# Replacing the scheduler's order by one written by hand in the first fifth of a fused attention and mixture-of-experts kernel

## The chip, the cores and the metric

The kernel runs on one NeuronCore of a Trainium2 chip. The metric is the device time of one execution in microseconds (us). PE is the matrix engine, DVE the vector engine, ACT the scalar engine, POOL the GpSimd engine, and SP the engine that only issues transfers. Each engine executes its own queue in order, and waits on semaphores for the others.

## The reference

Eight batches (B) of 512 tokens (S) and a state of 32 rows (Ns), with 8 heads (H) of 64 columns (D). The tokens read the state, the state reads the tokens, and the 8 x 544 rows go through 8 experts (E) with 1024 hidden columns (F), all experts for all rows, weighted by a matrix P that eight Sinkhorn rounds normalise:

```python
a = softmax(scale * x @ state.T)        # per batch and head: (512, 32)
xread = a @ state
a2 = softmax(scale * state @ x.T)       # (32, 512)
sread = a2 @ x
X = concatenate([xread, sread], axis=2) # as (4352, 512) rows
P = exp(X @ w_gate - max)
for _ in range(8):
    P /= P.sum(1, keepdims=True) + 1e-09
    P /= P.sum(0, keepdims=True) + 1e-09
    P *= N / E
out = sum over e of P[:, e:e+1] * (maximum(X @ w1[e], 0) @ w2[e])
```

## The kernel before

**Attention, in halves.** A batch's eight heads are done as two groups of four (`q` = 0, 1; in the code NQ = 2). The 16 groups are called heads below. For one head, PE transposes x (8 matmuls of 128 columns into `xT_ps`), DVE copies them out (`xT`), PE makes the scores (2 of 512 columns, `sc_ps`), ACT takes the exponential (`E2`, with its row sums), PE sums over state rows (`den_ps`), ACT makes the reciprocal with Ln and Exp (`rcp`), DVE divides the rows (`rrec`, `En`), PE transposes `En` (`ET_ps`), DVE copies that (`ET`) and multiplies `AT`, the weights with which tokens read the state, and PE reads x with `ET` (`su_ps`), which DVE copies to `xs`. `AT` and `xs` are all that the rest needs: X itself is never formed. `gate` multiplies a batch's `AT` with state x gate weights and ACT takes the exponential into `Pmat`.

**Expert 0.** For a pair of batches, `state_times_w1` forms state x W1 (8 matmuls into `g_ps`, each copied out in two halves to `G`). `layer1(c)` multiplies `G` with `AT` of batch c (8 steps of 2 matmuls into `hps`; ACT writes `hT` with Relu), `layer2(0, c)` multiplies `hT` with W2 (4 tiles of 8 matmuls into `yps`, copied to `acc`). c = 8 stands for the 256 state rows.

**Sinkhorn and experts 1 to 7.** A Sinkhorn round is a chain: four DVE instructions on `Pmat` that end in `cpart`, one small matmul (`csb_ps`), two DVE instructions. It can start only when all batches have been through `gate`. After it, `acc` (34 tiles) is multiplied by column 0 of `Pmat` (line 348), and experts 1 to 7 add to it. Their second layer is a seven-product (Winograd) scheme: `w2_sums` makes four sums of W2 (`wt`), `sums` four sums of `hT` (`sm`), and each product's tile (`ra`, `rb`, `rc`) is added to `acc` by DVE with a factor from `Pmat` (line 364).

**What sets the order.** The program is written phase by phase: all attention, Sinkhorn, expert 0, experts 1 to 7, with `merge` interleaving steps of two layers. The tile framework then schedules: it tracks every dependency, places tiles in pools, and interleaves the phases on each engine by its own priorities. SBUF is shared in time: the second weight buffer `moe_w1` is a pool opened after the attention pools are closed (`actx.close()`, line 255), so the load of expert 1's weights waits for the last head. PSUM has 8 banks: 4 for attention (`psA`) and 4 for the experts (`psM`), later all 8 (`psW`). Transfers of x and state go by SP's queue, transfers of weights by POOL's, which casts to 16 bits on the way; POOL also casts x of batches 1 to 7 (line 96), DVE that of batch 0.

Of the kernel before, what the change touches and what calls it, by code (L numbers as in the profile page):

```python
# [18 lines left out]
def kernel(  # L19
# [32 lines left out]
    mw = [ctx.enter_context(tc.tile_pool(name="moe_w0", bufs=1)), None]  # L52
    mh = ctx.enter_context(tc.tile_pool(name="moe_h", bufs=3))
# [32 lines left out]
    load_state(0)  # L86

    def load_x(b):
        x_nat = axp.tile([128, NKC, NSC, 2, D], FP16, name="x_nat", tag="x_nat")
        xv = x[b].rearrange("h (p s) d -> p h s d", s=NSC)  # L90
        for q in range(NQ):
            x_st = axs.tile([128, 4, NSC, D], FP32, name="x_st", tag="x_st")
            nc.sync.dma_start(out=x_st, in_=xv[:, ds(4 * q, 4)])
            for par in range(2):
                eng = nc.vector if b == 0 else nc.gpsimd
                eng.tensor_copy(out=x_nat[:, 2 * q + par].rearrange("p s i d -> p i s d"),
                                in_=x_st[:, ds(2 * par, 2)])
        return x_nat

    def load_w(e, after=None):  # L100
        w1h = mw[e % 2].tile([128, NKC, F], FP16, name="w1h", tag="w1h")
        w2h = mw[e % 2].tile([128, NFB, Dm], FP16, name="w2h", tag="w2h")
        for g in range(2):
            fs = ds(F // 2 * g, F // 2)
            if after is not None and g == 0:

                nc.gpsimd.tensor_copy(out=w1h[:1, 0, :1], in_=after[:1, 0, 0, 0, :1])
            nc.gpsimd.dma_start(out=w1h[:, :, fs], in_=w1r[e, :, :, fs])
# [18 lines left out]
    identh = consts.tile([128, 128], FP16, name="identh")  # L127
    make_identity(nc, identh)
    headones = consts.tile([128, 128], FP16, name="headones")
    nc.vector.memset(headones, 0.0)  # L130
    for h in range(4):
        nc.vector.memset(headones[ds(32 * h, 32), ds(32 * h, 32)], 1.0)
    nc.gpsimd.memset(stT, 0.0)
    ones128 = consts.tile([128, 128], FP32, name="ones128")
    nc.gpsimd.memset(ones128, 1.0)
    wgh = consts.tile([128, NKC, E], FP16, name="wgh")
    nc.gpsimd.dma_start(out=wgh, in_=moe_w_gate.rearrange("(kc p) e -> p kc e", p=128))

# [15 lines left out]
    x_nats = [load_x(0)]  # L154
    prepare_state(0)
    w_cur = load_w(0, x_nats[0])
    load_state(1)
    x_nats.append(load_x(1))

    def attention(b):  # L160
        xn = x_nats[b]
        odd = b % 2
        for q in range(NQ):
            xT_ps = psA.tile([128, 2, S], FP16, name="xT_ps", tag="a")
            for par in range(2):
                for sc in range(NSC):
                    nc.tensor.transpose(xT_ps[:, par, ds(128 * sc, 128)],
                                        xn[:, 2 * q + par, sc, :, :], identh)
            xT = asb.tile([128, 2, S], FP16, name="xT", tag="xT")
            nc.vector.tensor_copy(out=xT, in_=xT_ps)  # L170
            sc_ps = psA.tile([128, S], FP32, name="sc_ps", tag="a")
            for par in range(2):
                nc.tensor.matmul(sc_ps[ds(64 * (par ^ odd), 64), :],  # L173
                                 stT[:, b // 2, 2 * q + par, par ^ odd, :], xT[:, par, :])
            E2 = asb.tile([128, S], FP16, name="E2", tag="E2")
            rowsum = asb.tile([128, 1], FP32, name="rowsum", tag="rowsum")
            nc.scalar.activation(out=E2, in_=sc_ps, func=AF.Exp, scale=inv_sqrt_d,
                                 accum_out=rowsum)
            den_ps = psA.tile([128, S], FP32, name="den_ps", tag="a")
            nc.tensor.matmul(den_ps, headones, E2)  # L180
            lnd = asb.tile([128, S], FP32, name="lnd", tag="lnd")
            nc.scalar.activation(out=lnd, in_=den_ps, func=AF.Ln)  # L182
            rcp = asb.tile([128, S], FP16, name="rcp", tag="rcp")
            nc.scalar.activation(out=rcp, in_=lnd, func=AF.Exp, scale=-1.0)
            rrec = asb.tile([128, 1], FP32, name="rrec", tag="rrec")
            nc.vector.reciprocal(out=rrec, in_=rowsum)
            En = asb.tile([128, S], FP16, name="En", tag="En")
            nc.vector.tensor_scalar(out=En, in0=E2, scalar1=rrec, scalar2=None, op0=ALU.mult)
            ET_ps = psA.tile([128, NSC, 128], FP16, name="ET_ps", tag="a")
            for sc in range(NSC):  # L190
                nc.tensor.transpose(ET_ps[:, sc, :], En[:, ds(128 * sc, 128)], identh)
            ET = asb.tile([128, NSC, 128], FP16, name="ET", tag="ET")
            nc.vector.tensor_copy(out=ET, in_=ET_ps)
            nc.vector.tensor_mul(AT[:, q, ds(b * S, S)], E2, rcp)
            su_ps = psA.tile([128, 2, 64], FP32, name="su_ps", tag="a")
            for par in range(2):
                for sc in range(NSC):
                    nc.tensor.matmul(su_ps[:, par, :], xn[:, 2 * q + par, sc, :, :],
                                     ET[:, sc, ds(64 * (par ^ odd), 64)],
                                     start=(sc == 0), stop=(sc == NSC - 1))  # L200
            for i in range(2):
                nc.vector.tensor_copy(
                    out=xs[ds(64 * i, 64), ds(2 * q, 2), ds(b * Ns, Ns)],
# [295 lines left out]
```

## Time and profile before

| | |
|---|---|
| runs, median (lowest to highest) | 826.42 us (825.89 to 826.93), n = 4 |
| profiled execution: time, span of the core | 826.72 us, 824.9 us |
| busy in the span: PE, DVE, ACT, POOL | 789.8, 627.1, 614.0, 44.8 us |
| chain that ended last | PE 82%, DVE 9%, ACT 4%, DMA 3% |
| bytes read from and written to HBM | 42.48 MB, 8.91 MB |

Times inside the profile count from the first instruction (0) to the last (824.9); the 1.8 us between that and 826.72 lie around them. "Busy" of PE is the time in which some matmul was under way: matmuls are pipelined, so a PE that is shown busy can still be waiting between two. In groups of instructions a row gives the line, engine, operation, output and inputs, shapes and count, then busy time and mean duration, then the idle time of the engine just before them and what ended it. In a timeline a row gives the start, the length and the engine, and in brackets the idle time before and its releaser.

### The profile page before, as it was taken

Reading aid. Unit: us, or ns where it says so; the run is one execution under the profiler, and the core shown is the slowest. Engines: PE = TensorE matmul, PEld = TensorE weight load, DVE = VectorE, ACT = ScalarE, POOL = GpSimd, SP = SyncE. Lnnn points to the kernel's source line nnn. Section 1 sums busy time; section 2 is a strip of 40 time slices with the busy share of each in tenths; the row PEclk is TensorE's granted clock in tenths of the full one; section 3 lists DMA queues with packets and bytes.
Section 4 is the critical chain, followed back from the end, with each engine's and each line's share of the span. In section 5 each row is a group of like instructions: output and inputs, shape, how many; then the busy total and the mean of one; then the engine's idle time right before and its main releaser. Section 6 shows DMA issues by size and latency. Waiting matters only on the chain.

```text
span 824.9 us, 14279 instructions
## 1 busy us (share of the span) xinstructions
PE 789.8 (96%) x5584; PEld 518.8 (63%) x5584; DVE 627.1 (76%) x1353; ACT 614.0 (74%) x1158; POOL 44.8 (5%) x70
## 2 busy tenths in 40 slices
PE   3999979999999999999999999999999999999997
PEld 1344433456767667776667666776667666776664
DVE  3565768868887888788877888788877988788873
ACT  2687845698886788778886788878886788778861
POOL 3322010100000000000000000000000000000000
PEclk9999999999999999999999999999999999999999
DMA  9730060150003300060003300060003300003223
GB/s 197 212 103 27 1 102 1 22 80 3 1 1 53 52 1 1 1 102 2 2 1 52 52 1 1 2 102 1 1 1 52 52 1 2 1 14 116 102 104 103
DMA packets 33108, 35.53 MB, mean 43 GB/s; under 512 B 4112, under 2 KB 28688, under 8 KB 33040
## 3 DMA queue, kind: packets, MB, share of 16 engines
q0 software_dynamic: 17424, 16.79, 13.3%
q1 hardware_dynamic: 15616, 17.83, 6.6%
q8 instruction: 43, 0.70, 0.4%
q14 instruction: 25, 0.20, 0.1%
HBM read 42.48 MB, written 8.91 MB: 62 GB/s over the span
## 4 chain that ended last, share of the span: by engine, by line
PE 82%; DVE 9%; ACT 4%; DMA 3%; issue 1%; POOL 0%; SPq 0%; POOLq 0%
PE hps L298 24%; PE ra L358 24%; PE rc L358 12%; PE yps L315 6%; PE g_ps L237 6%; PE rb L358 5%; PE hps L303 2%; ACT hT L305 2%; DMA w2h<-in_moe_w_dram 1%; DMA w1h<-in_moe_w_dram 1%; DVE acc L364 1%; DVE sm L342 1%; DVE G L240 1%; PE sc_ps L173 1%; ACT lnd L182 1%
## 5 line engine op out<-in xcount | busy, mean ns | idle before, releaser
L305 ACT ACTIVATE hT<-hps 128x512 f16<-128x512 f32 (+1 forms) x576 | 306.7, 574 | 91.7 <-PE hps L298 62.6
L240 ACT CAST G<-g_ps 64x512 f16<-64x512 f32 x480 | 276.8, 577 | 65.2 <-PE g_ps L237 62.4
L298 PE MATMUL hps<-AT,G 128*128 128x512 f16 x1024 | 281.4, 383 | 2.0 <-ACT G L240 1.0
L364 DVE SCALAR_TENSOR_TENSOR acc<-ra,Pmat,acc 128x256 f32<-128x256 f32 x464 | 217.6, 479 | 46.7 <-PE ra L358 46.2
L358 PEld LDWEIGHTS <-sm 128*128 128x128 f16 x1856 | 178.9, 97 | 76.6 <-issue 14.8
L358 PEld LDWEIGHTS <-hT 128*128 128x128 f16 x1392 | 135.8, 98 | 51.3 <-issue 5.8
L298 PEld LDWEIGHTS <-G 128*128 128x128 f16 x1024 | 100.0, 99 | 72.7 <-issue 6.9
L358 PE MATMUL ra<-wt,sm 128*128 128x256 f16 x928 | 139.2, 272 | 3.2 <-DVE acc L364 2.4
L364 DVE SCALAR_TENSOR_TENSOR acc<-rc,Pmat,acc 128x256 f32<-128x256 f32 x232 | 111.5, 480 | 38.3 <-PE rc L358 38.2
L237 PE MATMUL g_ps<-w1h,stT 128*128 128x512 f16 x256 | 97.7, 388 | 5.0 <-DMA w1h<-in_moe_w_dram 3.9
L315 PE MATMUL yps<-w2h,hT 128*128 128x512 f16 x320 | 79.4, 382 | 0.6 <-ACT hT L305 0.4
L358 PE MATMUL ra<-w2h,hT 128*128 128x256 f16 x464 | 75.2, 273 | 0.0
L358 PE MATMUL rc<-wt,sm 128*128 128x256 f16 x464 | 70.6, 273 | 0.0
L358 PE MATMUL rb<-w2h,hT 128*128 128x256 f16 x464 | 69.7, 273 | 0.0
L358 PE MATMUL ra<-wt,hT 128*128 128x256 f16 x464 | 69.4, 272 | 0.0
L358 PE MATMUL rc<-w2h,sm 128*128 128x256 f16 x464 | 69.4, 271 | 0.0
L364 DVE SCALAR_TENSOR_TENSOR acc<-rb,Pmat,acc 128x256 f32<-128x256 f32 x116 | 55.6, 479 | 6.0 <-PE hps L298 0.5
L344 DVE TENSOR_TENSOR sm<-hT 128x1024 f16<-128x1024 f16 (+1 forms) x61 | 40.5, 663 | 15.3 <-ACT hT L305 15.1
L341 DVE TENSOR_TENSOR sm<-hT 128x1024 f16<-128x1024 f16 (+1 forms) x61 | 40.2, 659 | 15.6 <-ACT hT L305 15.6
L315 PEld LDWEIGHTS <-hT 128*128 128x128 f16 x320 | 29.9, 100 | 31.6 <-issue 2.8
L342 DVE TENSOR_TENSOR sm<-sm,hT 128x1024 f16<-128x1024 f16 (+1 forms) x61 | 39.9, 654 | 0.0
L343 DVE TENSOR_TENSOR sm<-hT,sm 128x1024 f16<-128x1024 f16 (+1 forms) x61 | 39.8, 652 | 0.0
(70 smaller groups left out, 389.8 us busy)
## 6 DMA issues: line engine op xcount, KB each, us to landing
x_st<-in_x_dram SPq DMA_DIRECT2D x16, 512.0 KB, 4.5
w1h<-in_moe_w_dram POOLq DMA_DIRECT2D x16, 512.0 KB, 7.1
w2h<-in_moe_w_dram POOLq DMA_DIRECT2D x16, 512.0 KB, 7.6
out_dram<-acc SPq DMA_DIRECT2D x32, 256.0 KB, 2.3
st_nat<-in_state_dram SPq DMA_DIRECT2D x8, 64.0 KB, 3.5
out_dram<-acc SPq DMA_DIRECT2D x8, 64.0 KB, 1.7
wgh<-in_moe_w_gate_dram POOLq DMA_DIRECT2D x1, 8.0 KB, 5.3
```

Source lines behind the costliest of these rows:

```text
L237: nc.tensor.matmul(g_ps, stT[:, bp, kc, :, :], w1h[:, kc, ds(512 * fh, 512)])
L240: evac(out=G[half ^ (kc % 2)][ds(64 * half, 64), kc // 2, ds(512 * fh, 512)], in_=g_ps[ds(64 * half, 64), :])
L298: nc.tensor.matmul(hps[:, :tn], G[:, q, ds(fb * 128, 128)], AT[:, q, ds(c * S, S)], start=(q == 0), stop=(q == NQ - 1))
L303: nc.tensor.matmul(hps[:, :tn], w1h[:, kc, ds(fb * 128, 128)], xs[:, kc, :], start=(kc == 0), stop=(kc == NKC - 1))
L305: nc.scalar.activation(out=hT[:, fb, :], in_=hps[:, :tn], func=AF.Relu)
L315: nc.tensor.matmul(yps, hT[:, fb, ds(tk * 128, 128)], w2h[:, fb, :], start=(fb == 0), stop=(fb == NFB - 1))
L341: nc.vector.tensor_add(s1, a21, a22)
L342: nc.vector.tensor_sub(s2, s1, a11)
L343: nc.vector.tensor_sub(s4, a12, s2)
L344: nc.vector.tensor_sub(s3, a11, a21)
L358: nc.tensor.matmul(r[nm], a[:, k, ds(128 * i, 128)], b[:, k, :], start=(first and k == 0), stop=(k == FH - 1), skip_group_check=True)
L364: nc.vector.scalar_tensor_tensor(out=dst, in0=r[nm], scalar=Pmat[:, t + i, e:e + 1], in1=dst, op0=ALU.mult, op1=ALU.add)
```

## The change

**A hand-written order.** From the first load to layer 1 of expert 1's batch 0, the code runs under `tc.manual_schedule` for all five engines: each engine's instructions stand in the order in which the code calls them. Attention becomes a class `Heads` with one method per stage, and `beat(k)` is the list of steps of one head, staggered with the next: (transposes of head k+1, row division of k), column sums of k, transposes of `En` of k, scores of k+1, (`AT` and x read of k). `weave` spreads one list of steps evenly in another; `units[c]` is layer 1 of batch c, layer 2 of batch c-1 (now in half tiles of 4 matmuls) and the next state x W1, and the beats of batch c+1 are woven into `units[c]`. Heads 0 and 1, and the whole of `prepare_state`, stand ahead of the first `g_ps`.

**Sinkhorn** stands in the tail of expert 0: its rounds are woven, one at a time, into layers 1 and 2 of batches 7 and 8, state x W1 of expert 1, and layer 1 of expert 1's batch 0.

**Smaller edits.** Weights get a pool of two buffers from the start (`moe_w`), `hT` gets two instead of three. Expert 1's weights are loaded while batch 4's attention runs. `G` of expert 0 is copied by DVE alone from the second batch pair on (half was ACT's). Ln writes in place in PSUM. x of batch 1 is cast by DVE. The first weight load waits for x's landing, not its cast. `w2_sums` is called after an expert's first batch, not before. `hT` and `G` are allocated at first use.

The core of the diff:

```diff
-    mw = [ctx.enter_context(tc.tile_pool(name="moe_w0", bufs=1)), None]
-    mh = ctx.enter_context(tc.tile_pool(name="moe_h", bufs=3))
+    mw = ctx.enter_context(tc.tile_pool(name="moe_w", bufs=2))
+    mh = ctx.enter_context(tc.tile_pool(name="moe_h", bufs=2))
...
+            (nc.vector if b < 2 else nc.gpsimd).tensor_copy(
+                out=x_nats[b][:, 2 * q + par].rearrange("p s i d -> p i s d"),
+                in_=x_st[b, q][:, ds(2 * par, 2)])
...
-            lnd = asb.tile([128, S], FP32, name="lnd", tag="lnd")
-            nc.scalar.activation(out=lnd, in_=den_ps, func=AF.Ln)
-            rcp = asb.tile([128, S], FP16, name="rcp", tag="rcp")
-            nc.scalar.activation(out=rcp, in_=lnd, func=AF.Exp, scale=-1.0)
+            nc.scalar.activation(out=den_ps, in_=den_ps, func=AF.Ln)
+            self.rcp = asb.tile([128, S], FP16, name="rcp", tag="rcp")
+            nc.scalar.activation(out=self.rcp, in_=den_ps, func=AF.Exp, scale=-1.0)
...
-                evac = nc.vector.tensor_copy if e == 0 and half else nc.scalar.copy
+                on_dve = e == 0 and (half or bp > 0)
+                evac = nc.vector.tensor_copy if on_dve else nc.scalar.copy
...
-    for b in range(B):
-        if 1 < b + 2 < B:
-            x_nats.append(load_x(b + 2))
-        attention(b)
-        if b == 0:
-            prepare_state(1)
-            state_times_gate()
-        gate(b * NSC, NSC)
-    gate(B * NSC, NTB - B * NSC)
+    manual.enter_context(tc.manual_schedule(engines={
+        mybir.EngineType.PE, mybir.EngineType.Activation, mybir.EngineType.DVE,
+        mybir.EngineType.Pool, mybir.EngineType.SP}))
+    heads = [Heads(k) for k in range(B * NQ)]
+    def beat(k):
+        h = heads[k]
+        n = heads[k + 1] if k + 1 < B * NQ and k + 1 != NQ else None
+        b, q = divmod(k, NQ)
+        return ([lambda: (n.transpose() if n else None, h.rows())] +
+                [h.columns, h.flip] + ([n.scores] if n else []) +
+                [lambda: (h.weights(), h.read_x())] +
+                ([lambda: gate(b * NSC, NSC)] if q else []))
...
+    def ahead(b):
+        if b < B:
+            load_x(b)
+            cast_x(b, 0)
+            cast_x(b, 1)
+        if b == B - 3:
+            w_nxt.extend(load_w(1))
...
+    prologue += [lambda: gate(B * NSC, NTB - B * NSC), sinkhorn_rows]
+    rest = [lambda: (sinkhorn_columns(), sinkhorn_rows()) for _ in range(7)] + [sinkhorn_columns]
+    Gs, first = state_times_w1(0, w1h, 0)
+    run(weave(first, [lambda: (cast_x(1, 0), cast_x(1, 1)), heads[2].transpose, heads[2].scores,
+                      lambda: gate(0, NSC)]))
...
+        units.append(weave(weave(last, l1), gs[4 * (c % 2):][:4]))
...
+    for c in range(B - 1):
+        run(weave(units[c], prologue[cut[c]:cut[c + 1]]))
+    actx.close()
...
-            merge(second, first)
+            if (e, c) == (1, 0):
+                tail = units[B - 1] + units[B]
+                tail = weave(tail[:4 * len(tail) // 5], second) + tail[4 * len(tail) // 5:]
+                run(tail[:6] + weave(tail[6:] + weave(units[B + 1], first), rest))
+                manual.close()
...
+            else:
+                run(weave(second, first))
+            if c == 0:
+                wt = w2_sums(e, w2h)
```

**What moves.** DVE's queue around one head of batch 2, before. Here the scheduler puts a `G` copy (line 240) between a head's first copies:

```order
L194 TENSOR_TENSOR AT<-E_380,rcp 128x512
L202 CAST xs<-su_ps 64x2x32 x2
L170 COPY xT<-xT_ps 128x1024
L240 CAST G<-g_ps 64x512
L186 RECIPROCAL rrec<-rowsum 128x1
L188 TENSOR_SCALAR En<-E_445,rrec 128x512
L193 COPY ET<-ET_ps 128x512
```

DVE's queue in the changed kernel around heads 2 and 3, in `units[0]` (names as above; `G` copies are line 249):

```order
L162 COPY xT<-xT_ps 128x1024
L177 RECIPROCAL rrec<-rowsum 128x1
L179 TENSOR_SCALAR En<-E_328,rrec 128x512
L249 CAST G<-g_ps 64x512 x2
L194 COPY ET<-ET_ps 128x512
L249 CAST G<-g_ps 64x512 x2
L197 TENSOR_TENSOR AT<-E_328,rcp 128x512
L208 CAST xs<-su_ps 64x2x32 x2
L162 COPY xT<-xT_ps 128x1024
L177 RECIPROCAL rrec<-rowsum 128x1
L179 TENSOR_SCALAR En<-E_411,rrec 128x512
```

The `G` copies now come in pairs, each pair directly ahead of a copy or product for which PE waits. DVE's queue where `acc` is first scaled, before:

```order
L272 SCALAR_TENSOR_TENSOR Pmat<-crec,Pmat 128x272
L318 COPY acc<-yps 128x512
L348 TENSOR_SCALAR acc<-acc,Pmat 128x512 x3
L318 COPY acc<-yps 128x512
L348 TENSOR_SCALAR acc<-acc,Pmat 128x512 x3
L318 COPY acc<-yps 128x512
L348 TENSOR_SCALAR acc<-acc,Pmat 128x512 x3
L318 COPY acc<-yps 128x512
L348 TENSOR_SCALAR acc<-acc,Pmat 128x512 x19
```

and in the changed kernel, from the last Sinkhorn round on (scaling is line 357, the adds of experts' products line 373):

```order
L270 SCALAR_TENSOR_TENSOR Pmat<-crec,Pmat 128x272
L357 TENSOR_SCALAR acc<-acc,Pmat 128x512 x2
L323 COPY acc<-yps 128x512
L357 TENSOR_SCALAR acc<-acc,Pmat 128x512 x2
L350 TENSOR_TENSOR sm<-hT 128x1024
L357 TENSOR_SCALAR acc<-acc,Pmat 128x512
L351 TENSOR_TENSOR sm<-sm,hT 128x1024
L373 SCALAR_TENSOR_TENSOR acc<-ra,Pmat,acc 128x256
L352 TENSOR_TENSOR sm<-hT,sm 128x1024
L373 SCALAR_TENSOR_TENSOR acc<-rb,Pmat,acc 128x256
L357 TENSOR_SCALAR acc<-acc,Pmat 128x512
```

Before, 28 of the 34 scalings stood in one piece among expert 0's last copies; now they stand one or two at a time between the sums and adds of expert 1's first five batches. POOL's queue from x's casts on, in the changed kernel (before, all 28 casts stood ahead of expert 1's first load):

```order
L102 CAST x_nat<-x_st 128x2x4x64 x16
L113 DMA w1h<-in_moe_w_dram 128x4x512 x2
L115 DMA w2h<-in_moe_w_dram 128x4x512 x2
L102 CAST x_nat<-x_st 128x2x4x64 x8
L113 DMA w1h<-in_moe_w_dram 128x4x512 x2
```

Expert 1's four loads moved ahead of the last eight casts.

297 lines of the change are left out of this document (169 added, 128 removed).

## The prediction

> **What bounds the kernel now.** I read the busy table by stages first, with the columns PE, weight loads, DVE, ACT, POOL (us and instructions), granted PE clock, DMA share and GB/s. The stages end at the first `g_ps` (19), the first `hps` (26.7), the last head (105), the end of the Sinkhorn stall (130), the first product of expert 1 (177.8), and one expert later.
>
> ```profile
> 0.00:19.00 19.00, 4.84 (x36) 3.19 (x37) 6.26 (x22) 3.96 (x9) 6.64 (x14) 1.00 1.00 192
> 19.00:26.70 7.70, 6.25 (x23) 1.86 (x23) 5.61 (x12) 5.77 (x12) 2.34 (x4) 1.00 0.84 210
> 26.70:105.00 78.30, 75.29 (x609) 36.23 (x610) 47.17 (x123) 58.79 (x130) 14.31 (x24) 1.00 0.23 75
> 105.00:130.00 25.00, 19.87 (x88) 8.49 (x87) 15.77 (x36) 12.03 (x25) 2.98 (x4) 0.86 0.54 85
> 130.00:177.80 47.80, 44.55 (x221) 21.09 (x220) 36.17 (x76) 30.91 (x62) 2.43 (x3) 1.00 0.14 22
> 177.80:270.30 92.50, 92.02 (x670) 64.87 (x669) 73.41 (x156) 74.65 (x138) 3.93 (x6) 1.00 0.16 24
> ```
>
> Experts 1 to 7 are PE-bound (92.02 of 92.50 us), so whatever is to be won lies before 177.8. There PE is also shown as nearly always busy, but a matmul that waits inside the pipeline counts as busy, so I weigh PE's work by the pace of an unhindered run, from the timeline of PE:
>
> ```profile
> 18.99 1.89 PE L237 MATMUL g_ps<-w1h,stT 128*128 128x512 f16 x4 [3.87 <-DMA w1h<-in_moe_w_dram]
> 26.74 4.45 PE L298 MATMUL hps<-AT,G 128*128 128x512 f16 x10 [0.94 <-DVE G L240]
> 34.02 1.24 PE L315 MATMUL yps<-w2h,hT 128*128 128x512 f16 x5
> ```
>
> The last row is the full pace: (1.24 - 0.38) / 4 = 0.215 us per 512-column matmul (one alone takes 0.38). The two rows above it run at 0.43, half pace, although the clock column says 1.00: until about 31.9 PE is slow, and the granted clock does not tell it. Matmuls of 26.74 to 177.79, by groups:
>
> ```profile
> L315 PE MATMUL yps<-w2h,hT 128*128 128x512 f16 x272 | 68.9, 383 | 0.6 <-ACT hT L305 0.4 <-DVE G L240 0.2
> L298 PE MATMUL hps<-AT,G 128*128 128x512 f16 x144 | 42.6, 408 | 2.0 <-ACT G L240 1.0 <-DVE G L240 0.9
> L237 PE MATMUL g_ps<-w1h,stT 128*128 128x512 f16 x36 | 13.0, 393 | 0.9 <-ACT hT L305 0.5 <-DVE G L240 0.4
> L167 PE MATMUL xT_ps<-identh,x_nat 128*128 128x128 f16 x112 | 9.3, 218 | 0.0
> L173 PE MATMUL sc_ps<-xT,stT 128*64 128x512 f16 x28 | 5.7, 399 | 1.4 <-DVE xT L170 1.3
> L191 PE MATMUL ET_ps<-identh,En 128*128 128x128 f16 x56 | 5.5, 221 | 0.0
> L198 PE MATMUL su_ps<-ET,x_nat 128*128 128x64 f16 x112 | 5.5, 192 | 0.6 <-DVE ET L193 0.6
> L180 PE MATMUL den_ps<-E,headones 128*128 128x512 f16 x14 | 5.3, 378 | 0.1
> L303 PE MATMUL hps<-xs,w1h 128*128 128x256 f16 x32 | 3.7, 273 | 0.0
> L269 PE MATMUL csb_ps<-cpart,ones 128*128 128x8 f32 x16 | 3.2, 275 | 6.3 <-DVE cpart L267 6.2
> ```
>
> 494 matmuls of 512 columns at 0.216 are 106.7 us; 168 of 128 columns at a quarter of that, 9.2; 32 of 256, 3.5; the 112 of 64 columns and some 110 smaller ones, about 6.4. That is 125.8 us of work in 151.05, so 25.2 us are lost. Of these I can name three. Slow pace from 26.74 to 31.9 costs half of 5.2, that is 2.6. The other two are one event, seen in POOL, DVE, PE and a clock row:
>
> ```profile
> 105.38 1.50 POOL L108 DMA_DIRECT2D w1h<-in_moe_w_dram  x2 [27.91 <-PE su_ps L198]
> ...
> 116.10 0.69 DVE L121 TENSOR_TENSOR wt<-w2h 128x1024 f16<-128x1024 f16 x1 [3.19 <-DMA w2h<-in_moe_w_dram]
> ...
> 118.63 0.69 DVE L122 TENSOR_TENSOR wt<-w2h 128x1024 f16<-128x1024 f16 x1 [1.02 <-DMA w2h<-in_moe_w_dram]
> ...
> 121.78 0.57 PE L269 MATMUL csb_ps<-cpart,ones 128*128 128x8 f32 x2 [4.57 <-DVE cpart L267]
> ...
> 122.00:124.00 2.00, 2.00 (x7) 0.90 (x8) 1.48 (x5) 0.00 (x0) 0.00 (x0) 0.50 0.00 0
> ```
>
> Expert 1's weights are asked for only after the last head's read of x; DVE, in order, sits on `wt` with the Sinkhorn chain behind it; PE, in order, sits 4.57 us on `csb_ps`; then its clock is 0.50, until about 127.5, for another 3.4 us lost. That leaves 25.2 - 2.6 - 4.6 - 3.4 = 14.6 us of small waits.
>
> **The change part by part.** The durations on DVE, from its groups in the same stretch, then single rows of DVE and POOL:
>
> ```profile
> L240 DVE CAST G<-g_ps 64x512 f16<-64x512 f32 x27 | 18.4, 693 | 3.4 <-ACT G L240 2.9
> L348 DVE TENSOR_SCALAR acc<-acc,Pmat 128x512 f32<-128x512 f32 x33 | 13.8, 476 | 0.2
> L170 DVE COPY xT<-xT_ps 128x1024 f16<-128x1024 f16 x14 | 9.7, 691 | 2.2 <-PE xT_ps L167 1.9
> L318 DVE COPY acc<-yps 128x512 f32<-128x512 f32 x14 | 9.6, 687 | 7.7 <-PE yps L315 7.7
> L194 DVE TENSOR_TENSOR AT<-E,rcp 128x512 f16<-128x512 f16 x14 | 5.9, 425 | 3.3 <-ACT rcp L184 3.2
> L193 DVE COPY ET<-ET_ps 128x512 f16<-128x512 f16 x14 | 5.9, 424 | 7.0 <-PE ET_ps L191 7.0
> L186 DVE RECIPROCAL rrec<-rowsum 128x1 f32<-128x1 f32 x14 | 2.3, 164 | 10.0 <-ACT E L177 9.9
> ...
> 6.80 0.76 DVE L96 CAST x_nat<-x_st 128x512 f16<-128x512 f32 x2 [5.33 <-DMA x_st<-in_x_dram]
> ...
> 14.30 0.46 DVE L202 CAST xs<-su_ps 64x64 f16<-64x64 f32 x2
> ...
> 153.44 6.80 DVE L348 TENSOR_SCALAR acc<-acc,Pmat 128x512 f32<-128x512 f32 x17
> ...
> 21.91 1.17 POOL L96 CAST x_nat<-x_st 128x512 f16<-128x512 f32 x2 [12.13 <-DMA x_st<-in_x_dram]
> ```
>
> *Start.* Heads 0 and 1 and the second half of the state now stand ahead of the first `g_ps` on PE. One head alone took from 6.80 to 14.76; the second overlaps it, and I put both, with the state's cast, at 18.3, and its copies and the gate's at 21.5 (estimates). So the wait for weights (18.99) is hidden by the heads. Then DVE has the first `G` copy, four casts of x (2 x 0.76), and with `xT` (0.69) four more `G` copies (0.69 each) before a bank is free for the first `hps`: about 27.9, against 26.74. Bounds: 25.5, if the heads overlap better; 31, if x of batch 1, now ahead of seven `G` copies on DVE, still lands as late as POOL saw it (21.91, and a second half after that). Its request is not later than before and state 1's, in front of it on SP's queue, is earlier, since the state's cast no longer waits for x: so 27.9. More is done by then: head 2's transposes and scores, the second state and one gate, 1.7 us of PE's work.
>
> *Unit 0.* 6.9 us of PE's work. DVE needs 4 x 2 x 0.69 for `G` and about 2.5 for each of two heads, some 10.5 us after a backlog of 2. I add 2.6 for the slow pace (as before) and 1.9 for DVE: 4.5.
>
> *Units 1 to 8 and the tail.* Everything else of the 125.8 is done unchanged. In a middle unit PE has about 14.5 us, DVE 8 x 0.69 + 2.3 x 2.5 = 11.3, ACT less than that, since `G`'s copies left it. Neither bounds. What is lost to waits in order lies between the rate of expert 1 (668 matmuls, 160 of 512 columns and 508 of 256, are 89.9 of 92.5 us: 2.9%, or 3.6 us here) and the 14.6 us that remained above. I take 5.5, near the low end, since a beat puts 1.3 to 2 us of other matmuls between each product and its use, about the 1.8 that DVE needs for two `G` copies and `ET`.
>
> *Sinkhorn.* The DMA wait, PE's idle 4.57 us and the half clock go: the weights are asked for three batches earlier, into a buffer of their own. The chain is now paced by the weave: the stretches of PE's work between two `csb_ps` are 3.0 to 3.9 us by matmul counts; DVE's round before takes 0.21 + 2 x 0.44 + 0.44 + 0.37 + 0.64, about 2.5, plus the trip to PE and one `acc` copy of 0.69. Mostly covered; where two copies fall into one round PE waits: 1.5 us in all (0 to 4).
>
> *Scaling.* In the old order 34 scalings at 0.40 (6.80 / 17), 13.6 us of DVE, stood beside expert 0's last matmuls. Now they stand in expert 1's first five batches. DVE is busy 73.41 of 92.50 there, about 8.6 per batch (4.5 for the state rows taken off, over 8); with 2.7 more, 11.3, against 10.7 of PE (20 x 0.216 + 56 x 0.109, and 2.9%). DVE becomes the bound by 0.6 x 5 = 3 us. Bounds: 0, if PSUM's eight banks carry it over; 8, if DVE also keeps its idle time in order.
>
> *At nothing:* `w2_sums` later in an expert (it had to wait for the old `wt`'s last use anyway), two `hT` buffers (batch c+2 begins after layer 2 of c), Ln in place, casts on DVE beside a PE that waits (in the start's sum), first-use allocation. Experts 2 to 7 and the end stay.
>
> Sum: 27.9 + (125.8 - 1.7) + 4.5 + 5.5 + 1.5 = 163.5 for the first product of expert 1, against 177.79: 14.3 less; 3 back in expert 1; 11.3 net. 824.9 - 11.3 + 1.8 = 815.4 us. The profiled execution's 826.72 is 0.3 above the median.
>
> **The rivals.**
>
> *Slow PE through unit 0.* From 18.99 to 26.7 PE was busy 6.25 of 7.70 us and stayed at half pace; it was released only after the dense run of `hps`. If DVE thins unit 0, the release may come at its end: 6.9 us of work take 13.8, to 41.7 instead of 39.3, so 817.8. [...]
>
> *The order by hand keeps the small waits.* Then 14.6 instead of 5.5 are lost: 824.5. For it: 7.0 and 10.0 us of DVE's idle time ahead of `ET` and `rrec` before, which a fixed order may hand on. Against it: those 17 us are over 14 heads in which head k+1 was not yet staggered.
>
> *Better.* DVE carries the scaling over (3), waits at expert 1's rate (1.9), start at 25.5 (2.4): 808.1.
>
> *Slower.* Each head's `ET` copy stands behind a pair of `G` copies (1.4 us) that cannot be passed; if the 1.8 us of that chain are not covered, PE's read of x waits in every head, and everything behind it. At 0.8 us per head, 14 heads eat the 11.3; at 1.2 the time is 815.4 + 16.8 = 832.2. For it: nothing may overtake now. Against it: the 1.3 to 2 us counted above.
>
> **How the numbers follow.** Forecast 815.4: 0.46; slow PE 0.12; better 0.15; small waits kept 0.15; slower 0.12. The range leaves out the slower case and little of the others: 807 to 825. A difference of 0.2% (1.7 us) is about what can be told from none. Faster by more: 0.46 + 0.12 + 0.15 + 0.11 of the fourth = 0.84; the same 0.04; slower 0.12.
>
> **What would show it.** First `hps` near 28; no idle time of PE over 2 us after 30 and no clock row under 1.00 between 40 and 800; expert 1's load issued by POOL before 95; the first product of expert 1 near 163; DVE over 90% busy in the 55 us after it, with expert 1 about 3 us longer than 92.5; later experts at 92.5. I am wrong if PE waits for `ET` or `G` copies in each beat, if x of batch 1 lands after 24, or if expert 1 loses 8 us.

## The result and the profile after

| | changed kernel | kernel before |
|---|---|---|
| median of the undisturbed runs (lowest to highest) | 808.25 us (807.64 to 808.90) | 826.01 us (824.95 to 827.46) |
| ratio, 95% interval | 0.9781 (0.9772 to 0.9791) | |
| profiled execution shown below: time, span | 807.49 us, 805.7 us | 826.72 us, 824.9 us |
| first `hps`, first product of expert 1 | 27.23, 158.88 us | 26.74, 177.79 us |

The change takes 17.8 us off. The forecast of 815.4 had the sign and the range right and was 7 us too high. The lines of the changed kernel are those of a second profiled execution, since the first fell in a disturbed run of 1996 us.

The busy table by stages, with the columns PE, weight loads, DVE, ACT, POOL, granted PE clock, DMA share and GB/s. The stages end at the first `g_ps`, the first `hps`, the end of unit 0 (the first `yps`), the last `su_ps` and its gate, the first product of expert 1, two stretches of expert 1, and the end of expert 2:

```profile
0.00:19.70 19.70, 8.39 (x71) 5.05 (x72) 9.03 (x33) 6.54 (x17) 6.83 (x14) 1.00 0.99 210
19.70:27.23 7.53, 5.36 (x32) 2.14 (x29) 6.31 (x15) 3.96 (x9) 1.39 (x3) 1.00 0.92 221
27.23:38.20 10.97, 8.85 (x76) 4.25 (x74) 10.50 (x24) 8.42 (x19) 3.93 (x8) 1.00 0.74 239
38.20:124.00 85.80, 85.80 (x629) 42.73 (x628) 59.25 (x131) 59.42 (x121) 11.47 (x19) 1.00 0.25 56
124.00:158.88 34.88, 32.74 (x177) 17.06 (x176) 31.09 (x68) 25.89 (x49) 2.99 (x4) 1.00 0.22 33
158.88:213.00 54.12, 53.95 (x388) 37.77 (x388) 52.01 (x120) 43.47 (x80) 0.00 (x0) 1.00 0.12 19
213.00:251.30 38.30, 37.90 (x283) 27.35 (x282) 29.68 (x64) 29.19 (x56) 2.65 (x4) 1.00 0.19 29
251.30:343.80 92.50, 92.05 (x670) 64.85 (x668) 75.23 (x159) 74.22 (x137) 2.86 (x5) 1.00 0.15 24
```

From 38.20 to 124 PE is busy without a gap, and no clock row is below 1.00. A matmul of 512 columns is shown for 0.38 us while the next can start 0.215 us behind it, so a wait of up to 0.16 us between two is shown as busy. So I count PE's matmuls at the prediction's prices: 0.216 us for 512 columns, a quarter of that for 128, and 6.4 / 222 = 0.029 us for a smaller one. By this estimate the 629 matmuls (341, 136 and 152 of the three kinds) are 85.4 us of work in 85.80. The old kernel's 568 matmuls from 35 to 105 us (225, 168 and 175) were 62.8 us of work in 70.00. The largest groups of the stretch in the changed kernel (the last figure is the idle time before them), then the old kernel's window:

```profile
L318 PE MATMUL yps<-w2h,hT 128*128 128x512 f16 x192 | 49.2, 379 | 0.0
L298 PE MATMUL hps<-AT,G 128*128 128x512 f16 x95 | 28.4, 379 | 0.0
L245 PE MATMUL g_ps<-w1h,stT 128*128 128x512 f16 x20 | 7.6, 382 | 0.0
```

```profile
35.00:105.00 70.00, 67.07 (x568) 32.70 (x566) 43.61 (x111) 53.37 (x118) 9.99 (x17) 1.00 0.17 54
```

In the tail, 124 to 158.88, these are all the waits of PE that the trace names (total, times, longest): the Sinkhorn chain is not among them. The longer one stands ahead of expert 1's first product: `ra` reads no `G`, so by the code it waits there for a bank of the new PSUM pool.

```profile
PE ra L367 <- ACT G L249: 1.7, 1, 1.7
PE g_ps L245 <- DVE acc L323: 0.4, 1, 0.4
```

POOL's timeline has expert 1's weights asked for 52 us earlier than before, so that nothing waits for them:

```profile
53.25 1.49 POOL L113 DMA_DIRECT2D w1h<-in_moe_w_dram  x2
54.73 1.50 POOL L115 DMA_DIRECT2D w2h<-in_moe_w_dram  x2
```

What is left stands in unit 0. PE's timeline, then DVE's:

```profile
27.23 1.06 PE L298 MATMUL hps<-AT,G 128*128 128x512 f16 x2
...
28.85 0.38 PE L184 MATMUL den_ps<-E,headones 128*128 128x512 f16 x1
29.07 0.59 PE L298 MATMUL hps<-AT,G 128*128 128x512 f16 x2
...
35.37 0.40 PE L192 MATMUL ET_ps<-identh,En 128*128 128x128 f16 x4 [1.28 <-DVE En L179]
```

```profile
31.80 1.38 DVE L249 CAST G<-g_ps 64x512 f16<-64x512 f32 x2
...
34.16 0.69 DVE L162 COPY xT<-xT_ps 128x1024 f16<-128x1024 f16 x1
...
34.96 0.35 DVE L179 TENSOR_SCALAR En<-E,rrec 128x512 f16<-128x512 f16 x1
```

Two `hps` matmuls take 1.06 us at 27.23 and 0.59 at 29.07: PE's pace doubles at about 28.5, with the clock column at 1.00 throughout. After that it is DVE that is late: busy 10.50 of 10.97 us, it makes `En` only at 34.96, and PE waits 1.28 us for it.

### The profile page after: what moved, and what is told of

It is laid out like the page before. It is cut to its first block, busy times and chain, and to the rows that moved or that the text cites. A ratio compares the mean times of both kernels' runs of the same rounds, so it can differ in the third digit from the quotient of the medians.

```text
span 1994.4 us, 14253 instructions
## 1 busy us (share of the span) xinstructions
PE 1976.0 (99%) x5584; PEld 913.7 (46%) x5584; DVE 680.2 (34%) x1381; ACT 637.3 (32%) x1134; POOL 41.6 (2%) x66
## 4 chain that ended last, share of the span: by engine, by line
PE 82%; DVE 0%; ACT 0%; issue 0%
PE ra L367 27%; PE hps L298 25%; PE rc L367 13%; PE rb L367 7%; PE g_ps L245 6%; PE hps L303 3%; PE yps L318 1%; DVE acc L326 0%; ACT G L249 0%
## 5 line engine op out<-in xcount | busy, mean ns | idle before, releaser
L298 PE MATMUL hps<-AT,G 128*128 128x512 f16 x1024 | 669.8, 801 | 0.0
L367 PEld LDWEIGHTS <-sm 128*128 128x128 f16 x1856 | 314.7, 170 | 326.5 <-issue 143.7
L367 PEld LDWEIGHTS <-hT 128*128 128x128 f16 x1392 | 237.9, 171 | 236.6 <-issue 108.1
L367 PE MATMUL ra<-wt,sm 128*128 128x256 f16 x928 | 319.7, 519 | 0.0
L245 PE MATMUL g_ps<-w1h,stT 128*128 128x512 f16 x256 | 207.3, 813 | 0.0
L318 PE MATMUL yps<-w2h,hT 128*128 128x512 f16 x320 | 198.4, 814 | 0.0
L367 PE MATMUL ra<-w2h,hT 128*128 128x256 f16 x464 | 166.6, 519 | 1.3 <-ACT G L249 1.3
L367 PE MATMUL rc<-wt,sm 128*128 128x256 f16 x464 | 160.2, 513 | 0.0
L367 PE MATMUL rb<-w2h,hT 128*128 128x256 f16 x464 | 159.3, 523 | 0.0
L367 PE MATMUL rc<-w2h,sm 128*128 128x256 f16 x464 | 158.9, 519 | 0.0
L318 PEld LDWEIGHTS <-hT 128*128 128x128 f16 x320 | 54.3, 171 | 118.3 <-issue 115.2
```

What stands on the lines that cost most here:

```text
L245: nc.tensor.matmul(g_ps, stT[:, bp, kc, :, :], w1h[:, kc, ds(512 * fh, 512)])
L298: nc.tensor.matmul(hps[:, :tn], G[c % 2][:, q, ds(fb * 128, 128)], AT[:, q, ds(c * S, S)], start=(q == 0), stop=(q == NQ - 1))
L318: nc.tensor.matmul(yps[tk], h[0][:, fb, ds(tk * 128, 128)], w2h[:, fb, :], start=(fb == 0), stop=(fb == NFB - 1))
L367: nc.tensor.matmul(r[nm], lhs[:, k, ds(128 * i, 128)], rhs[:, k, :], start=(first and k == 0), stop=(k == FH - 1), skip_group_check=True)
```

## The experiments

All are compared with the old kernel's runs on the same chip; differences "to the changed kernel" are to its 808.25. "First product" is that of expert 1. late_w, no_stagger, act_g and early_g ran on another chip than the other runs of the table; the old kernel's median was 825.48 us there, and 825.22 to 826.33 on the first chip.

| run | us | ratio to before (95%) | first `hps` | first `yps` | first product |
|---|---|---|---|---|---|
| changed kernel once more (a_again) | 807.49 | one run | 27.23 | 38.20 | 158.88 |
| pools_only | 820.77 | 0.9939 (0.9924 to 0.9953) | 26.98 | 32.34 | 171.90 |
| pools_stagger | 817.97 | 0.9909 (0.9896 to 0.9923) | 24.52 | 31.30 | 168.32 |
| late_w | 817.22 | 0.9890 (0.9868 to 0.9912) | 27.28 | 38.95 | 168.39 |
| no_stagger | 820.83 | 0.9939 (0.9917 to 0.9962) | 27.68 | 41.56 | 173.44 |
| free_order | 811.82 | 0.9829 (0.9812 to 0.9845) | 32.59 | 40.85 | 164.00 |
| free_guard | 812.28 | 0.9840 (0.9827 to 0.9854) | 32.84 | 41.10 | 163.86 |
| no_scaling | 807.89 | 0.9782 (0.9768 to 0.9797) | 27.98 | 39.34 | 160.02 |
| act_g | 810.26 | 0.9809 (0.9785 to 0.9832) | 27.67 | 40.70 | 162.04 |
| early_g | 809.10 | 0.9796 (0.9771 to 0.9820) | 27.93 | 39.05 | 159.72 |
| pool_cast | 806.12 | 0.9767 (0.9754 to 0.9780) | 25.24 | 36.87 | 157.56 |
| early_state | 804.96 | 0.9754 (0.9739 to 0.9768) | 23.79 | 35.18 | 155.86 |

**The changed kernel once more (a_again).** The changed kernel, unaltered.

> The changed kernel once more, for its profile. By the prediction's steps: first hps near 28, first product of expert 1 near 163, expert 1 about 95.5 us long instead of 92.5, time 808 (as measured, 7 less than forecast). Rival for the missing 7: expert 1 is no longer than 92.5 (3 of the 7) and the rest is fewer waits before it, so that its first product stands near 160.

Measured: 807.49; its profile is the one above. The rival is right: expert 1 takes 92.4 us (158.88 to 251.30), and its first product stands at 158.88.

**The early load alone (pools_only).** The old kernel with the new weights' pool, two `hT` buffers and the early request:

```diff
-    mw = [ctx.enter_context(tc.tile_pool(name="moe_w0", bufs=1)), None]
-    mh = ctx.enter_context(tc.tile_pool(name="moe_h", bufs=3))
+    mw = ctx.enter_context(tc.tile_pool(name="moe_w", bufs=2))
+    mh = ctx.enter_context(tc.tile_pool(name="moe_h", bufs=2))
...
-            w_nxt = load_w(1)
+            w_nxt = load_w(1, x_nats[B - 3])
```

> The kernel before with only two weight buffers from the start, and expert 1's weights asked for after batch 5's cast; the scheduler's order. Theory: the stall at the end of attention (4.6 us idle, 3.4 us at half clock) goes and nothing else: 826.0 - 8 = 818. Rival: the Sinkhorn chain stays exposed on DVE and takes the stall's place: 822 to 826.

Measured: 820.77, 5.6 us less than before, between the two. The stall and the half clock behind it are gone, but the small waits of the old order stay. A stretch of half clock now stands at the first `hps`, where the old kernel was at half pace too:

```profile
26.00:28.00 2.00, 1.01 (x3) 0.43 (x4) 1.99 (x5) 0.69 (x2) 0.96 (x2) 0.64 1.23 214
28.00:30.00 2.00, 2.00 (x7) 0.62 (x5) 1.18 (x3) 1.43 (x3) 0.22 (x1) 0.50 1.17 250
```

From 32.30 to 171.90 us every clock row is 1.00. Its windows, from the first `yps` to the last gate, through the Sinkhorn rounds, and to the first product:

```profile
32.30:105.00 72.70, 69.30 (x583) 33.51 (x582) 45.18 (x115) 55.42 (x124) 15.36 (x26) 1.00 0.31 90
105.00:140.20 35.20, 31.35 (x153) 13.44 (x152) 30.77 (x66) 19.59 (x40) 0.00 (x0) 1.00 0.00 1
140.20:171.90 31.70, 30.20 (x155) 14.99 (x156) 21.06 (x46) 22.94 (x46) 2.03 (x3) 1.00 0.21 34
```

PE is idle 3.4, 3.85 and 1.5 us there; in the changed kernel, from unit 1 to the first product, 0 and 2.1. Of the 3.85 us, 2.6 are waits of `csb_ps` for the Sinkhorn chain.

**The early load undone (late_w).** The changed kernel, with expert 1's weights asked for after the last read of x:

```diff
-        if b == B - 3:
-            w_nxt.extend(load_w(1))
...
+                 lambda: (w_nxt.extend(load_w(1, xs[:1, 3, N - B * S - 1:N - B * S])), sinkhorn_rows())]
```

> The changed kernel, but expert 1's weights are asked for where the old kernel asked for them: after the last head's read of x (about 121 us), instead of during batch 4's attention. Buffers, order and weave stay. Theory (the early request is a term of its own: without it PE, in its fixed order, meets expert 1's first g_ps about 3 us after the request, while two halves of w1h need about 6 us each to land): PE idle 3 to 6 us ahead of g_ps in 124 to 131 us, a clock row of 0.50 behind it if the idle time is near 4.6 us, and in all 3 to 8 us more than 808.3, so 811 to 816 us. Rival (the Sinkhorn rounds no longer stand behind w2_sums on DVE, and that alone removed the old stall; the request's time is then worth nothing): 807.5 to 809.5 us, PE idle under 1.5 us there.

Measured: 817.22, 9.0 us more than the changed kernel; the theory's direction, and more than its upper end. PE's timeline has two waits where the theory had one, and DVE's says what the second is: `wt`, which the scheduler puts among the Sinkhorn rounds although the code calls it behind them, waits for w2h, and the chain stands behind it on DVE, as in the old kernel. (In the changed kernel `wt` stands ahead of the rounds too, but its weights have long landed.)

```profile
129.25 0.38 PE L245 MATMUL g_ps<-w1h,stT 128*128 128x512 f16 x1 [2.89 <-DMA w1h<-in_moe_w_dram]
...
139.83 0.39 PE L267 MATMUL csb_ps<-cpart,ones 128*128 128x8 f32 x2 [2.21 <-DVE cpart L263]
```

```profile
134.31 0.69 DVE L126 TENSOR_TENSOR wt<-w2h 128x1024 f16<-128x1024 f16 x1 [2.24 <-DMA w2h<-in_moe_w_dram]
```

The windows show a slow stretch behind each, a row out of each stretch:

```profile
130.00:132.00 2.00, 2.00 (x8) 0.67 (x6) 0.63 (x1) 1.42 (x3) 0.00 (x0) 0.59 1.24 205
...
142.00:143.00 1.00, 1.00 (x4) 0.37 (x3) 0.97 (x3) 0.25 (x1) 0.00 (x0) 0.50 0.00 0
```

In 2 us windows the clock reads 0.59 and 0.55 from 130 to 134, in 1 us windows 0.81, 0.50, 0.50, 0.50 and 0.99 from 140 to 145: 1.72 and 1.70 us short of 1.00. With 2.89 and 2.21 us of idle time that is 8.5 of the 9.5 us by which the first product is later. The early request is a part of the gain of its own, and Sinkhorn's place did not make it superfluous.

**The stagger alone (pools_stagger).** pools_only with attention written in staggered heads, and the old scheduler's order:

```diff
-        attention(b)
+        for k in (2 * b, 2 * b + 1):
+            n = heads[k + 1] if k + 1 < B * NQ else None
+            if n:
+                n.transpose()
+            heads[k].rows()
+            heads[k].columns()
+            heads[k].flip()
+            if n:
+                n.scores()
+            heads[k].weights()
+            heads[k].read_x()
```

> The old kernel with two parts of the change alone: the weights' pool of two buffers with expert 1's load beside batch 5 (worth 5.6 us by itself), and the attention written staggered (head k+1's transposes ahead of head k's row division, its scores ahead of head k's AT and read of x). The scheduler keeps setting the order; Sinkhorn, scaling and the rest stand where they stood. Theory (stagger and early load are the two halves of the 18.2 us: 5.6 and, by the run without stagger, 12.6): 807 to 812 us. Rival (the scheduler reorders heads anyway, so that the code's stagger tells it little; what the hand-written order needs the scheduler does not): 818 to 822 us, as with the pools alone. Between the two: the rest lies in Sinkhorn's place and the half tiles.

Measured: 817.97, at the rival's lower end: 2.8 us beyond the pools. The first `hps` comes 2.5 us earlier, but the first `yps` only 1.0. Behind it most of the loss stays. From the first `yps` on, by windows:

```profile
31.30:79.00 47.70, 44.81 (x464) 23.65 (x463) 38.16 (x105) 38.94 (x91) 15.54 (x26) 1.00 0.47 140
79.00:111.00 32.00, 29.34 (x155) 12.81 (x152) 27.87 (x61) 19.47 (x40) 0.00 (x0) 1.00 0.00 1
```

Attention now runs ahead to 79 us, with DVE busy 38.16 of 47.70 us. PE is idle 2.9 us in the first stretch and 2.7 in the second; 1.9 of the 2.7 are waits of `csb_ps` for the Sinkhorn chain, which the tail of the changed kernel does not have.

**The stagger undone (no_stagger).** The changed kernel, each head's steps by themselves:

```diff
-        return ([lambda: (n.transpose() if n else None, h.rows())] +
-                [h.columns, h.flip] + ([n.scores] if n else []) +
-                [lambda: (h.weights(), h.read_x())] +
+        return ([lambda: h.transpose() if k > NQ else None] +
+                [lambda: h.scores() if k > NQ else None] +
+                [lambda: (h.rows(), h.columns()), h.flip, lambda: (h.weights(), h.read_x())] +
```

> The changed kernel, but a beat is one head alone: transposes, scores, (row division, column sums), transposes of En, (AT, x read), with no step of head k+1 ahead of head k's. It is woven into the same units, five steps per head as before. Theory (the small waits went from 14.6 to about 3.4 us because the stagger puts other matmuls between each product and its use): the chain scores, Exp, 1/rowsum, En, transposes has a fixed latency near 2.5 us that one step of a unit (about 1.4 us of PE) does not cover, so PE waits 0.5 to 1.5 us at one or two places in each of 14 heads: 7 to 25 us more, 815 to 833 us. Rival (any even weave with layer 1 and layer 2 covers it, the stagger is not needed): 807 to 811 us.

Measured: 820.83, 12.6 us more. The theory is right. The waits of PE from 41.5 to 138, in which the changed kernel has none (total, times, longest):

```profile
PE sc_ps L168 <- DVE xT L162: 3.7, 7, 0.6
PE den_ps L184 <- ACT E L172: 2.3, 5, 0.5
PE su_ps L204 <- DVE ET L194: 1.5, 5, 0.3
PE ET_ps L192 <- DVE En L179: 0.6, 1, 0.6
```

They are 8.1 us, in each link of a head's chain. Unit 0 is longer too, 13.88 us instead of 10.97, with a stretch of half pace in it (two `hps` take 0.59 us at 36.99 and 1.06 at 38.79):

```profile
27.68:41.56 13.88, 10.65 (x65) 4.58 (x64) 11.00 (x24) 7.94 (x17) 4.54 (x9) 0.88 0.58 189
```

With the two runs before: the new order without the stagger (820.83) is worth no more than the pools alone (820.77), the stagger in the old order 2.8 us, and the two together 12.5. The waits in a head's chain go only with the pair. But the new order is a package: it holds Sinkhorn's place, the half tiles and the smaller edits as well as the weave, and no run takes these apart. Nor does a run show what the scheduler would have made of the woven code without the stagger.

**The order left to the scheduler (free_order, free_guard).** The changed kernel without the lines that fix the order; then also with expert 1's first load behind a one-element copy of batch 5's x:

```diff
-    manual.enter_context(tc.manual_schedule(engines={
-        mybir.EngineType.PE, mybir.EngineType.Activation, mybir.EngineType.DVE,
-        mybir.EngineType.Pool, mybir.EngineType.SP}))
...
-            w_nxt.extend(load_w(1))
+            w_nxt.extend(load_w(1, x_nats[b][:1, 0, 0, 0, :1]))
```

> The changed kernel's code without the manual schedule: the scheduler may again reorder on every engine. Theory (what counts is that the phases are woven in the code and the weights come early, since the scheduler follows the code's order where it can): 808 to 813. Rival (the order by hand is what removes the small waits): 817 to 822, only the stall of 8 us gone.

> The changed code with the order left to the scheduler (811.8 us before, with first hps at 32.59), and expert 1's first load now made to wait for batch 5's cast x by a one-element copy, so that it cannot be asked for at 10 us beside expert 0's weights. Theory (the 3.6 us between free and hand order are the start alone, where expert 1's 2 MB share the queue with what the first hps needs): first hps at 27 to 29, 807.5 to 809.5 us. Rival (expert 1's load at 10 us is no harm, the scheduler's order of expert 0's own halves is, second half of w1h first): first hps at 31 to 33, 811 to 813 us.

Measured: 811.82, the theory's, and 812.28, the rival's. From the first `hps` to the first product the scheduler needs 131.4 us, the hand order 131.65: given code that is written woven, it makes no worse of it. The difference is the start. PE's timeline of free_order, then DVE's:

```profile
20.84 1.46 PE L245 MATMUL g_ps<-w1h,stT 128*128 128x512 f16 x3 [5.96 <-DMA w1h<-in_moe_w_dram]
22.10 0.63 PE L192 MATMUL ET_ps<-identh,En 128*128 128x128 f16 x4
```

```profile
22.77 0.42 DVE L194 COPY ET<-ET_ps 128x512 f16<-128x512 f16 x1 [7.63 <-PE ET_ps L192]
```

The scheduler puts the first `g_ps` on PE ahead of head 1's transposes of `En` and of the state's second half. Its wait for w1h, which the hand order fills with just these, now holds them up, and DVE behind them. POOL's timeline of free_guard:

```profile
3.97 0.75 POOL L113 DMA_DIRECT2D w1h<-in_moe_w_dram  x1
...
7.01 1.18 POOL L115 DMA_DIRECT2D w2h<-in_moe_w_dram  x1
8.18 0.87 POOL L113 DMA_DIRECT2D w1h<-in_moe_w_dram  x1
```

The half of w1h that the first `g_ps` needs is asked for third. That alone does not make the start late: pools_stagger asks for the halves in the same order and has its first `hps` at 24.52. POOL's and PE's timelines of pools_stagger:

```profile
8.18 0.75 POOL L108 DMA_DIRECT2D w1h<-in_moe_w_dram  x1
```

```profile
18.96 1.03 PE L257 MATMUL g_ps<-w1h,stT 128*128 128x512 f16 x2 [4.48 <-DMA w1h<-in_moe_w_dram]
```

The guard held only one of expert 1's four transfers (the others were still asked for at 9.8 to 12 us), so its run does not settle whether these transfers do harm too. pools_stagger asks for three of them as early (from 9.65 us on), which speaks against it. Why w1h lands about 2 us later here than there stays open.

**The scaling (no_scaling).** Expert 0's share isn't weighted at all:

```diff
-            if e == 1:
+            if False:
```

> The changed kernel without the 34 multiplications of acc by column 0 of Pmat (expert 0's share stays unweighted). Theory: they make DVE the bound in expert 1's first five batches, 3 us: 805. Rival: PSUM's banks carry them over, within 0.5 us of the changed kernel, 808.

Measured: 807.89, the same as with it. The rival is right. The window that answers to 158.88 to 213 above:

```profile
160.00:214.20 54.20, 54.18 (x390) 37.78 (x390) 42.99 (x91) 44.47 (x80) 0.00 (x0) 1.00 0.12 20
```

DVE has 42.99 us to do instead of 52.01, so 30 scalings add about 0.3 us each in place, and PE does 390 matmuls in 54.20 us instead of 388 in 54.12.

**`G`'s copies back to ACT (act_g).**

```diff
-                on_dve = e == 0 and (half or bp > 0)
+                on_dve = e == 0 and half
```

> The changed kernel, but one half of each G copy of expert 0's batch pairs 1 to 3 goes back to ACT, as in the old kernel (27 fewer copies become 12 fewer on DVE: 12 x 0.69 = 8.3 us move from DVE to ACT between 27 and 120 us). In unit 0 DVE was busy 10.53 of 11.0 us and ACT 8.45. Theory (DVE's load and the pairs of G copies ahead of ET are no bound outside unit 0; in unit 0 the bound goes over to ACT, 8.45 + 2.8): between -1 and +1.5 us, 807 to 810 us. Rival (the hand order lives from an ACT that is free for Relu and Exp): 1 us more in each of units 0 to 5, 812 to 815 us. Second rival (DVE was the bound in more than unit 0): 804 to 806.5 us.

Measured: 810.26, 2.0 us more: the theory's place (unit 0, where ACT becomes late), 0.3 us beyond its upper end; neither rival. Unit 0 is 13.03 us long instead of 10.97, units 1 to 7 are not longer (85.7), and PE waits longer for the same `En`:

```profile
27.67:40.70 13.03, 10.69 (x75) 5.18 (x74) 8.75 (x21) 10.13 (x23) 4.73 (x9) 0.87 0.62 201
```

```profile
36.63 0.40 PE L192 MATMUL ET_ps<-identh,En 128*128 128x128 f16 x4 [2.34 <-DVE En L179]
```

The clock of 0.87 is a slow stretch behind that wait (0.66, 0.50, 0.50 and 0.63 in the 1 us windows from 37 to 41), and 0.13 of 13.03 us, 1.7 us, is what it costs.

**A better start, in three versions.** early_g weaves the first state x W1 with the rest of head 1, the state's second half and the gate's product, instead of placing it behind them; pool_cast lets POOL cast x of batch 1; early_state does both and moves the state's second half up into head 0:

```diff
 (pool_cast, early_state)
-            (nc.vector if b < 2 else nc.gpsimd).tensor_copy(
+            (nc.vector if b < 1 else nc.gpsimd).tensor_copy(
...
 (early_state)
+    Gs, first = state_times_w1(0, w1h, 0)
     heads[1].scores()
+    prepare_state(1)
     heads[0].weights()
     heads[0].read_x()
     heads[1].rows()
     heads[1].columns()
     heads[1].flip()
+    run(first[:2])
     heads[1].weights()
     heads[1].read_x()
-    prepare_state(1)
+    run(first[2:4])
     state_times_gate()
+    run(first[4:5])
+    cast_x(1, 0)
+    cast_x(1, 1)
+    heads[2].transpose()
+    run(first[5:])
+    heads[2].scores()
+    gate(0, NSC)
...
-    Gs, first = state_times_w1(0, w1h, 0)
-    run(weave(first, [lambda: (cast_x(1, 0), cast_x(1, 1)), heads[2].transpose, heads[2].scores,
-                      lambda: gate(0, NSC)]))
```

> The changed kernel, but the first state x W1 (8 g_ps) is woven with the second half of head 1, the second half of the state, the gate's product and head 2's transposes, instead of standing behind all of them. The weights' halves landed at 13.8 and 18.0 us in the profile of the changed kernel, where the first g_ps stands at 19.70 and the first hps at 27.23. Theory (the start is bound by the order on PE and DVE and no longer by a transfer; DVE has 9.6 us of copies and casts between 14.0 and the first hps beside its 1.3 us waits): first g_ps near 15.5, first hps near 25, 2 us less in all: 805 to 807 us. Rival (DVE's backlog sets unit 0 anyway, and what is gained at the first hps is lost by 38 us): 807.5 to 809 us. Second rival (x of batch 1, late, or PE's slow pace sets it): first hps at 27 or later, 808 to 810 us.

> The changed kernel, but x of batch 1 is cast by POOL (idle from 8.9 to 25 us) instead of DVE, as in the old kernel. Theory (DVE sets the start from 14 us on and unit 0, 10.53 of 11.0 us busy): the 1.43 us go, 806.5 to 807.5 us. Rival (PE's half pace or the second half of w1h sets the first hps): 807.8 to 809 us.

> A version meant to beat both: the changed kernel with a new order of the start. The state's second half is cast, transposed and copied inside head 0 (it landed at 9.4 us, and DVE had idle time of 0.7 us three times there), the first two state x W1 products stand inside head 1, two more behind it, the gate's product after them, and x of batch 1 is cast by POOL. In the earlier try (early_g, first hps 27.9) the state's copies were late: t_ps at 19.46 behind a DVE that had two G copies ahead of it, ACT's copies at 20.8, G copies of 22.2 behind those. Theory (that jam is all that kept the early g_ps from paying, and DVE's 1.43 us of casts go too): first hps near 24.5, 803.5 to 806.5 us. Rival (the second half of w1h, which lands at 18.0 us or later, and the half pace set it): first hps 26 to 27, 806.5 to 808 us.

Measured: early_g 809.10, the second rival, and not to be told from the changed kernel's time: the first `g_ps` came 4 us earlier, the first `hps` 0.7 later. PE's timeline of early_g shows what the new order made late, the state's cast and x's, both behind `G` copies on DVE:

```profile
19.46 0.61 PE L137 MATMUL t_ps<-identh,st_h 128*128 128x128 f16 x4 [2.52 <-DVE st_h L134]
...
24.02 1.03 PE L159 MATMUL xT_ps<-identh,x_nat 128*128 128x128 f16 x8 [2.24 <-DVE x_nat L102]
```

pool_cast 806.12: 2.1 us less than the changed kernel, more than the 1.43 us of casts and 0.4 us below the theory's range. early_state 804.96: theory, 3.3 us less than the changed kernel, with an interval that lies below the changed kernel's. Its median is the lowest of all, though its interval overlaps that of pool_cast. Its windows of unit 0 and of units 1 to 7, and pool_cast's of the latter:

```profile
23.80:35.20 11.40, 9.65 (x81) 4.97 (x78) 10.26 (x24) 8.23 (x19) 4.53 (x9) 0.85 0.89 268
35.20:121.00 85.80, 85.80 (x629) 42.69 (x628) 59.25 (x131) 59.39 (x121) 11.49 (x20) 1.00 0.25 58
```

```profile
36.90:122.70 85.80, 85.80 (x629) 42.71 (x628) 59.25 (x131) 59.39 (x121) 11.47 (x20) 1.00 0.26 56
```

The 629 matmuls take 85.80 us in all three: after unit 0 nothing but PE's own pace is left, and what is won at the start arrives at the end.

## Why the prediction was right in direction and 7 us too high

| step | forecast | measured | by which run |
|---|---|---|---|
| first `hps` | 27.9 | 27.23 | changed kernel |
| unit 0 | 6.9 + 4.5 = 11.4 | 10.97 | changed kernel |
| waits, unit 1 to the first product | 5.5 + 1.5 = 7.0 | 120.68 - 117.2 = 3.5 | changed kernel |
| first product of expert 1 | 163.5 | 158.88 | changed kernel |
| scaling in expert 1 | +3.0 | 0 (251.30 - 158.88 = 92.4) | no_scaling |

- **Mis-sized: the scaling, by 3 us.** The step that failed is "DVE becomes the bound by 0.6 x 5": a batch with 11.3 us on DVE against 10.7 on PE. The 2.7 us per batch for scaling came from scalings in a row, 0.40 us each; in place, among DVE's idle times, they add about 0.3 us each, and four of the 34 stand ahead of that stretch. Measured, DVE is busy 52.01 of 54.12 us (96%), it keeps 2 us of slack, and PE loses nothing. no_scaling shows it by taking 9 us off DVE there without effect.
- **Mis-sized: the waits, by 3.5 us.** The 5.5 for small waits rested on expert 1's rate and on `G` pairs ahead of `ET`. In units 1 to 7 PE waits for nothing. The 1.3 to 2 us of other matmuls that a beat puts between a product and its use do cover the chain; no_stagger shows that the stagger is needed for it. Of Sinkhorn's 1.5 nothing is seen as a wait for `cpart`; 2.1 us of idle time in the tail stand elsewhere, 1.7 of them ahead of expert 1's first product. The other 1.4 of the 3.5 are no wait that the trace names.
- **Two readings were off without moving the sum much.** The half clock before lasted from 120.7 to 127.5 (0.67, 0.50, 0.50 and 0.63 in the 2 us windows from 120 to 128), but PE was idle until 121.78, so it cost half of 5.7, about 2.9 and not 3.4; 15.1 us of small waits were left, not 14.6. And at the prediction's own prices unit 0 has about 7.6 us of PE's work, not 6.9. The 125.8 hold the difference, so the sum stays, but then 3.4 us are lost in unit 0 and 4.2 behind it; the table goes by the 6.9.
- **Right: the load.** The DMA wait, the idle 4.57 us and the 0.50 are gone, and late_w brings them back with 9.0 us.
- **Right in size, partly in cause: unit 0.** The 4.5 us lost were split into 2.6 for the pace and 1.9 for DVE. The pace doubled at 28.5 instead of 31.9, so the slow stretch took half of 1.3, about 0.6. Waits for DVE took 2.1 (1.8 for `En`, 0.3 for `ET`). The rest of the 4.1 us (10.97 - 6.9) is not placed.
- **Right: the start**, within 0.7 us, with x of batch 1 not late (DVE's casts of it waited for no transfer). That DVE's casts cost there is shown by pool_cast.
- **The rivals.** "Better" is what happened, at its own 808.1: two of its three conditions hold (scaling carried over, waits near expert 1's rate), the third, a start at 25.5, does not. That it met the number is partly luck: waits 1.6 us below its own (3.5 against 3.6 + 1.5), a first `hps` 0.7 us earlier than 27.9 and a unit 0 shorter by 0.4 made up for the 2.4 us of that start. "The order by hand keeps the small waits" and "slower" fell; no_stagger, at 820.83, comes nearest to the first. "Slow PE through unit 0" did not occur here; what lifts the pace, no run shows. act_g, no_stagger and early_state show something near it: once at full pace, their PE fell back inside unit 0, to a clock of 0.50 in the windows of act_g and early_state, and to 1.06 us for two `hps` in no_stagger.

## What to carry to other kernels

A chain that hops between engines is hidden by giving the in-order engine other work in each gap: behind unit 0 PE waited 8.1 us in its chains without the stagger, with it not at all. Here that took both a stagger of the chain's iterations and a new order that spreads them in independent work: the stagger alone brought 2.8 us, the new order alone nothing, both 12.5. An engine at 96% load beside a bound engine cost nothing here, because the added work fell into its idle time; so price such work by the idle time that it finds, and not by the difference of two averages. A wait with a slow stretch behind it is priced with that stretch: in late_w two idle periods of 2.89 and 2.21 us cost 8.5 us, not 5.1.

## What the runs showed of the hardware that was not expected

**Pauses of 1.7 to 2.9 us stood ahead of stretches at half clock.** In early_state PE's timeline has, at 23.23, a wait of 1.71 us. The 1 us windows from 24 to 28 behind it have clocks of 0.52, 0.50, 0.50 and 0.78, 1.70 us short of 1.00. The wait, and two of the windows:

```profile
23.23 0.41 PE L168 MATMUL sc_ps<-xT,stT 128*64 128x512 f16 x2 [1.71 <-DVE xT L162]
```

```profile
24.00:25.00 1.00, 1.00 (x8) 0.73 (x7) 1.00 (x2) 0.83 (x4) 0.02 (x1) 0.52 1.18 243
...
26.00:27.00 1.00, 1.00 (x4) 0.32 (x3) 0.96 (x4) 0.64 (x2) 0.00 (x0) 0.50 1.10 362
```

Slow stretches also stood behind 2.34 us in act_g (1.71 us short, by its windows) and behind 2.89 and 2.21 us in late_w (1.72 and 1.70 us short), but not behind 1.28 us in the changed kernel, 1.74 us ahead of its first product, or a second wait in early_state, of 1.70 us at 32.34, where the windows to 36 read 1.00. Shorter pauses came before a slow stretch, too: in no_stagger, whose pace has halved by 38.79, no single pause from 28 us to there is over 1.26 us. So the length of one pause does not tell whether a slow stretch follows; what does, no run shows.

**The granted clock does not show the slow start.** It reads 1.00 while two 512-column matmuls take 1.06 us here (at 27.23; 0.59 at 29.07) and ten take 4.45 us before (at 26.74; 16 take 3.62 at 152.45), until about 28.5 us here and 31.9 before; only the durations tell.
